# Last 512-token tile's second layer: other buffers for squares and reciprocals, and the older block's quotient ahead of the newer block's polynomials

## The chip, the core and the metric

The kernel runs on one core of a Trainium2 chip. The engines are PE (TensorE, matrix products), DVE (VectorE), ACT (ScalarE), POOL (GpSimd) and SP (which issues the transfers). Each works through its own queue in order, and they meet at semaphores. The metric is the device time of one launch in microseconds (us).

## What is computed

An attention without softmax (squared ReLU of the scores) gives 6016 rows of 256 values. A first feed-forward layer with ELU follows, and then the second one, whose activation is a rational function of the hidden value h. The change touches this last part:

```python
h = x @ w_in                       # 256 -> 2048
P = a[0] + a[1]*h + a[2]*h2 + a[3]*h3
Q = 1.0 + abs(b[0])*abs(h) + abs(b[1])*h2
g = P / (Q + 1e-06)
return g @ w_out                   # 2048 -> 256
```

## The kernel before

Tokens of the two feed-forward layers are taken in 13 tiles: one of 384, ten of 512 and two of 256 (`NFT` is 13, so tile `NFT - 3`, number 10 counted from 0, is the last with 512 tokens). The hidden dimension of 2048 is cut into blocks of 128 hidden units by up to 512 columns: a 512-token tile has 16 blocks, and a 256-token tile has 8, each with two groups of hidden units side by side. Every product is made of three matmuls on a high and a low part, so each block of either layer costs PE six matmuls of 512 columns for the hidden values (`hidden`, L358 to L361) and six for the projection (`mm3`, L239 to L241), or twelve and twelve of 256 columns.

`ffn_step(n)` writes the instructions of one step in a fixed order, and nothing rearranges them later. In the steps here, PE works on the first layer of tile 11 (every second step) while the second layer of tile 10 goes through, one block per step, in several stages: `second_hidden(j)` in one step, the polynomials of that block (`j1`) in the next, its reciprocal and quotient (`j2`) in the step after, its projection (`j4`) two steps later. I call `j2` the older block and `j1` the newer one, and number the blocks of tile 10 from 0 to 15. A step with a first-layer block I call a full step, one without it a half step.

Tile 10 uses the form "spread" of the activation:

- ACT: `linear` (L431), `square` (L439), `size` (L448), all from h in PSUM; later `recip`, a logarithm (L471) and an exponential (L472).
- POOL: `cubic` (L451), from linear and square; later `rest` (L485), the low part of the result. POOL also makes the low part of the first layer's block (L398).
- DVE: `denominator` (L457), from square and size; `numerator` (L465), from cubic; `quotient` (L478, L479, L480); and for the first layer `first_elu` (L391).

The buffers matter. Square and reciprocal of a block live in the two halves of one `raw` buffer, from `square` until `rest` has read the reciprocal. There are three `raw` buffers, and `load_x1` keeps one for the input of the last tile, from the step of the third first-layer block of tile 11 until `split_x1` in the step of its eighth. `e` (three buffers) holds the first layer's exponentials, and `r` (two) the reciprocals of the other tiles. The eight PSUM banks hold four accumulators and up to four hidden blocks; a block of the second layer frees its bank when its quotient is done, one of the first layer when its ELU is done.

After the last step, `finish` writes the last tile's second layer in an order that it plans itself; the change leaves that alone.

Of the kernel before, what the change touches and what calls it, by code (L numbers as in the profile page):

```python
# [16 lines left out]
def f(ap):  # L17
    return ap.bitcast(F32)
# [3 lines left out]
def attention_then_two_ffns(  # L22
# [51 lines left out]
    NFT = len(ftiles)  # L74
# [11 lines left out]
    def sb(tag, bufs, dt=F32, name=None):  # L86
        return sp.tile([P, W], dt, tag=tag, bufs=bufs, name=name or tag)

    def bank(name):
        return ps.tile([P, W], F32, tag="bank", name=name)  # L90
# [43 lines left out]
    def load_raw():  # L134
        return sp.tile([P, 2, 2 * P, 2], U32, tag="raw", bufs=3, name="raw")
# [187 lines left out]
    def load_x1(ti):  # L323
        t0, w = ftiles[ti]
        x1[ti] = load_raw().rearrange("p k f t -> p k (f t)").bitcast(F32)
        for sp_, (bb, i0, ws) in enumerate(spans):
            c0 = bb * S + i0
            lo, hi = max(c0, t0), min(c0 + ws, t0 + w)
            if lo < hi:
                nc.sync.dma_start(out=x1[ti][:, :, lo - t0:hi - t0], in_=xd[sp_][:, :, lo - c0:hi - c0])  # L330
# [11 lines left out]
    def flat(i):  # L342

        return PER[i[0]] * widths[i[0]]
# [34 lines left out]
    def first_hidden(i):  # L379
        g1[i] = hidden(0, x1[i[0]], i)  # L380

    def first_exp(i):
        h = g1[i]
        e = sb("e", 3)[:, :flat(i)]
        nc.scalar.activation(e, h, AF.Relu, scale=-1.0)
        nc.scalar.activation(e, e, AF.Exp, scale=-1.0)  # L386
        g1[i] = e, h

    def first_elu(i):
        e, h = g1[i]  # L390
        nc.vector.scalar_tensor_tensor(out=e, in0=e, scalar=-1.0, in1=h, op0=ALU.add, op1=ALU.max)  # L391
        g1[i] = e
# [8 lines left out]
    def split_x2(ti):  # L401
        w = widths[ti]
        x2[ti] = []
        for d in range(ND):
            p = acc[0, ti][d][:, :w]
            hi, lo = (sb("x2", 4, F32R)[:, :w] for _ in range(2))
            nc.scalar.copy(hi, p)
            nc.vector.tensor_tensor(out=lo, in0=p, in1=f(hi), op=ALU.subtract)
            x2[ti].append((hi, lo))

    def second_hidden(i):
        mid[i] = {"h": hidden(1, x2[i[0]], i)}

    def second(i, form):

        st = mid[i]  # L420
        h, n = st["h"], flat(i)
        last, plain = form == "last", form == "plain"
        v, act, tt, stt = nc.vector, nc.scalar.activation, nc.gpsimd.tensor_tensor, nc.vector.scalar_tensor_tensor

        def new(key, tag, bufs, dt=F32):
            t = wp.tile([P, W], dt, tag="w", name=tag) if last else sb(tag, bufs, dt)
            st[key] = t[:, :n]
            return st[key]

        def linear():  # L430
            act(new("p", "t", 3), h, AF.Identity, bias=a2, scale=a3)  # L431

        def square():
            if last:
                new("s", "s2", 0), new("r", "r", 0)
            else:
                raw = load_raw().rearrange("p k f t -> p k (f t)").bitcast(F32)
                st["s"], st["r"] = raw[:, 0, :n], raw[:, 1, :n]
            act(st["s"], h, AF.Square)  # L439

        def size():
            if last:
                st["q"] = bank("q")[:, :n]
            else:
                new("q", "q", 3)
            if plain:
                new("r", "r", 2)
            act(st["q"], h, AF.Abs, scale=b1 if plain else b0)  # L448

        def cubic():  # L450
            tt(out=st["p"], in0=st["p"], in1=st["s"], op=ALU.mult)  # L451

        def denominator():
            if plain:
                stt(out=st["q"], in0=st["q"], scalar=b0, in1=h, op0=ALU.add, op1=ALU.mult)  # L455
            else:
                stt(out=st["q"], in0=st["s"], scalar=b1, in1=st["q"], op0=ALU.mult, op1=ALU.add)  # L457

        def numerator():
            if plain:  # L460
                v.tensor_tensor(out=st["p"], in0=st["p"], in1=h, op=ALU.mult)
                stt(out=st["p"], in0=st["p"], scalar=a1, in1=h, op0=ALU.add, op1=ALU.mult)
                st["top"] = st["p"]
            else:
                stt(out=h, in0=h, scalar=a1, in1=st["p"], op0=ALU.mult, op1=ALU.add)  # L465
                st["top"] = h

        def recip():
            if plain:
                act(st["q"], st["q"], AF.Abs)  # L470
            act(st["r"], st["q"], AF.Ln, bias=NQ * LNS, scale=LNS)  # L471
            act(st["r"], st["r"], AF.Exp, bias=LNB, scale=-1.0)  # L472

        def quotient():

            new("hi", "x", 6, F32R)
            prod = st["q"] if plain else st["s"]
            stt(out=st["hi"], in0=st["top"], scalar=a0, in1=st["r"], op0=ALU.add, op1=ALU.mult)  # L478
            stt(out=prod, in0=st["q"], scalar=NQ, in1=f(st["hi"]), op0=ALU.add, op1=ALU.mult)  # L479
            stt(out=st["p"], in0=st["top"], scalar=a0, in1=prod, op0=ALU.add, op1=ALU.subtract)  # L480

        def rest():

            new("lo", "x", 6, F32R)
            tt(out=st["lo"], in0=st["p"], in1=st["r"], op=ALU.mult)  # L485
            g2[i] = st["hi"], st["lo"]

        if plain:
            return [
                ("linear", "A", 1.1, ["hidden"], linear),  # L490
                ("size", "A", 1.0, ["hidden"], size),
                ("denominator", "V", 1.0, ["size"], denominator),
                ("numerator", "V", 2.0, ["linear"], numerator),
                ("recip", "A", 2.6, ["denominator"], recip),
                ("quotient", "V", 3.0, ["recip", "numerator"], quotient),
                ("rest", "G", 1.8, ["quotient"], rest),
            ]
        return [
            ("square", "A", 0.85, ["hidden"], square),
            ("size", "A", 1.0, ["hidden"], size),  # L500
            ("linear", "A", 1.1, ["hidden"], linear),
            ("denominator", "V", 1.0, ["square", "size"], denominator),
            ("cubic", "G", 1.8, ["square", "linear"], cubic),
            ("recip", "A", 1.75, ["denominator"], recip),
            ("numerator", "V", 1.0, ["cubic"], numerator),
            ("quotient", "V", 3.0, ["recip", "numerator"], quotient),
            ("rest", "G", 1.8, ["quotient"], rest),
        ]

    def form(i):  # L510

        return "spread" if i[0] == NFT - 3 or i[0] == 0 and i[1] < 2 else "plain"

    def second_steps(i, *names):
        ops = mid[i].setdefault("ops", {x[0]: x[-1] for x in second(i, form(i))})
        for name in names:
            if name in ops:
                ops[name]()
# [32 lines left out]
    def ffn_step(n):  # L551
        i, i1, p = begun.get(n), begun.get(n - 1), projected.get(n)
        j, j1, j2, j4 = (second_begun.get(n - k) for k in (0, 1, 2, LAG2))
        last = p is not None and p[1] == NG[p[0]] - 1
        if i and i[1] * PER[i[0]] == 4 and i[0] + 1 < NFT:
            load_x1(i[0] + 1)

        if last and j:
            second_hidden(j)
        if p:  # L560
            project(0, p, g1.pop(p))
        if i:
            first_hidden(i)
        if j1:
            second_steps(j1, "linear", "square", "size", "cubic", "denominator")
            if form(j1) == "plain":
                second_steps(j1, "numerator")
        if i1:
            first_elu(i1)
        if i and i[1] == NG[i[0]] - 1 and i[0] + 1 < NFT:  # L570
            split_x1(i[0] + 1)
        early = n < LAG1 + NG[0] + 2
        if i1 and early:
            first_split(i1)
        if j2:
            second_steps(j2, "recip")
        if last:
            split_x2(p[0])
        if i:
            first_exp(i)  # L580
        if j2:
            second_steps(j2, "quotient", "rest")
        if j1 and form(j1) != "plain":
            second_steps(j1, "numerator")
        if i1 and not early:
            first_split(i1)
        if j4:
            second_project(j4)
            if j4[1] == NG[j4[0]] - 1:
                store(j4[0])  # L590
        if not last and j:
            second_hidden(j)
# [90 lines left out]
    first = stages_z(0, 0, True, True, False)  # L683
# [74 lines left out]
```

## Time and profile before

| | |
|---|---|
| median of 3 runs | 1644.72 us (1644.67 to 1645.53) |
| the profiled execution | 1644.66 us |
| its span, first to last instruction | 1642.9 us |
| PE busy | 97% of the span |
| DVE, ACT, POOL busy | 87%, 82%, 42% |
| mean granted TensorE clock | 0.993 |

The profiled execution is within 0.1 us of the median, and 1.8 us of it lie outside the span. In the trace, a row of an engine's timeline has its start, its duration, the engine, the line of the program, the operation, what it writes and reads, and in brackets how long the engine had been idle before it and what ended that. Matmuls are pipelined, so their work is read from the distance between starts. Instructions of DVE and ACT overlap their neighbours by up to 0.1 us too; so here again a cost in a row of instructions is the distance of two starts, and the duration counts where another engine waits for the end.

### The profile page before, as it was taken

To read this page: it belongs to the slowest core of one execution; us is meant where nothing else is said; L and a number is where in the kernel's file an instruction comes from. 1 tells how busy PE (TensorE), PEld (TensorE's weight loads), DVE (VectorE), ACT (ScalarE), POOL (GpSimd) and SP (SyncE) were. 2 spreads that over 40 slices of the span, in tenths; PEclk is the share of its full clock that TensorE was granted. 3 is DMA by queue.
4 is the path that set the end of the run, shared out by engine and by line. 5 is a ranking of instruction groups with operands and counts; after the bars stand their busy time and mean duration, and the time that the engine had idled before them with its cause. 6 is when DMAs were issued, how large, how long until landed. Compare 5 with 4: busy or idle time off the path is not lost.

```text
span 1642.9 us, 21580 instructions
## 1 busy us (share of the span) xinstructions
PE 1596.4 (97%) x7272; PEld 1312.4 (80%) x7272; DVE 1424.3 (87%) x2184; ACT 1342.0 (82%) x2297; POOL 687.9 (42%) x547
## 2 busy tenths in 40 slices
PE   8999999999999999999999999999999999987896
PEld 6888888888889988878788787878787878876796
DVE  8888889999997478898888989898989888896888
ACT  7777787878876788888898888888888989875786
POOL 3223230323322444444444445444445444454645
PEclk9999999999999999999999999999999999998999
DMA  4133333221221500000000000000000000000000
GB/s 128 62 119 104 115 117 111 84 82 61 70 84 60 165 14 1 23 1 27 1 26 1 26 1 1 26 1 26 1 27 0 20 1 20 1 2 12 1 14 14
DMA packets 42191, 67.72 MB, mean 41 GB/s; under 512 B 6112, under 2 KB 19168, under 8 KB 42080
## 3 DMA queue, kind: packets, MB, share of 16 engines
q1 hardware_dynamic: 42080, 66.34, 12.9%
q8 instruction: 57, 0.93, 0.3%
q14 instruction: 54, 0.44, 0.1%
HBM read 47.71 MB, written 18.61 MB: 40 GB/s over the span
## 4 chain that ended last, share of the span: by engine, by line
PE 81%; DVE 9%; ACT 4%; issue 3%; POOL 2%; DMA 0%; POOLq 0%; SPq 0%; DVEq 0%; ACTq 0%
PE acc L240 16%; PE acc L241 16%; PE acc L239 16%; PE h L358 9%; PE h L361 9%; PE h L359 9%; PE s L264 4%; PE s L263 4%; DVE x L478 2%; POOL x L485 1%; DVE e L391 1%; DVE t L480 1%; ACT q L448 1%; PE acc L301 1%; DVE s L273 1%
## 5 line engine op out<-in xcount | busy, mean ns | idle before, releaser
L485 POOL TENSOR_TENSOR x<-t,r 128x512 fp32r<-128x512 f32 (+1 forms) x174 | 222.6, 1279 | 475.3 <-DVE t L480 453.8
L398 POOL TENSOR_TENSOR lo<-e,hi 128x512 fp32r<-128x512 f32 (+1 forms) x192 | 246.8, 1286 | 25.5 <-ACT hi L397 23.3
L266 ACT ACTIVATE e<-s 128x512 f32<-128x512 f32 (+1 forms) x288 | 169.0, 587 | 92.1 <-PE s L264 87.2
L273 DVE SCALAR_TENSOR_TENSOR s<-s,e 128x512 f32<-128x512 f32 (+1 forms) x280 | 191.5, 684 | 46.5 <-ACT e L266 43.1
L431 ACT ACTIVATE t<-h,coef 128x512 f32<-128x512 f32 (+1 forms) x192 | 148.0, 771 | 86.9 <-PE h L361 86.8
L455 DVE SCALAR_TENSOR_TENSOR q<-q,coef,h 128x512 f32<-128x512 f32 (+1 forms) x166 | 122.1, 736 | 83.1 <-ACT q L448 82.9
L358 PE MATMUL h<-x,w 128*128 128x512 f32 (+2 forms) x416 | 156.5, 380 | 14.2 <-DVE t L480 13.2
L240 PE MATMUL acc<-x,w 128*128 128x512 f32 (+2 forms) x416 | 157.2, 378 | 9.6 <-POOL x L485 9.4
L240 PE MATMUL acc<-lo,w 128*128 128x512 f32 (+2 forms) x416 | 157.2, 378 | 2.9 <-POOL lo L398 2.6
L239 PE MATMUL acc<-x,w 128*128 128x512 f32 (+2 forms) x416 | 156.1, 375 | 3.2 <-ACT xo L531 3.2
L358 PE MATMUL h<-rl,w 128*128 128x512 f32 (+2 forms) x416 | 154.5, 375 | 4.4 <-DVE e L391 3.9
L239 PE MATMUL acc<-hi,w 128*128 128x512 f32 (+2 forms) x416 | 156.2, 376 | 0.0
L241 PE MATMUL acc<-x,w 128*128 128x512 f32 (+2 forms) x416 | 156.2, 375 | 0.0
L241 PE MATMUL acc<-hi,w 128*128 128x512 f32 (+2 forms) x416 | 155.8, 374 | 0.0
L359 PE MATMUL h<-x,w 128*128 128x512 f32 (+2 forms) x416 | 155.4, 377 | 0.0
L359 PE MATMUL h<-rl,w 128*128 128x512 f32 (+2 forms) x416 | 153.3, 372 | 0.0
L391 DVE SCALAR_TENSOR_TENSOR e<-e,h 128x512 f32<-128x512 f32 (+1 forms) x192 | 128.5, 669 | 23.8 <-ACT e L386 23.8
L397 ACT CAST hi<-e 128x512 fp32r<-128x512 f32 (+1 forms) x192 | 115.3, 600 | 34.1 <-DVE e L391 34.0
L478 DVE SCALAR_TENSOR_TENSOR x<-t,coef,r 128x512 fp32r<-128x512 f32 (+1 forms) x166 | 133.7, 806 | 0.1
L240 PE MATMUL acc<-lo,v 128*128 128x512 f32 (+1 forms) x334 | 130.9, 392 | 0.6 <-DVE lo L286 0.5
L448 ACT ACTIVATE q<-h,coef 128x512 f32<-128x512 f32 (+1 forms) x192 | 129.1, 672 | 2.4 <-DVE s L479 2.4
L239 PE MATMUL acc<-hi,v 128*128 128x512 f32 (+1 forms) x334 | 130.5, 391 | 0.0
(107 smaller groups left out, 4293.5 us busy)
## 6 DMA issues: line engine op xcount, KB each, us to landing
raw<-w_in_dram SPq DMA_DIRECT2D x16, 512.0 KB, 4.2
raw<-w_out_dram SPq DMA_DIRECT2D x16, 512.0 KB, 4.6
wd<-q SPq DMA_DIRECT2D x24, 256.0 KB, 2.2
raw<-wd SPq DMA_DIRECT2D x12, 512.0 KB, 3.4
raw<-v_dram SPq DMA_DIRECT2D x22, 256.0 KB, 3.3
raw<-uT_dram SPq DMA_DIRECT2D x10, 512.0 KB, 4.1
xd<-xo SPq DMA_DIRECT2D x20, 256.0 KB, 2.4
outT_dram<-xo SPq DMA_DIRECT2D x20, 256.0 KB, 2.2
```

Source lines behind the costliest of these rows:

```text
L239: nc.tensor.matmul(out, lhsT=lh, rhs=rh, start=start, stop=False)
L240: nc.tensor.matmul(out, lhsT=lh, rhs=rl, start=False, stop=False)
L241: nc.tensor.matmul(out, lhsT=ll, rhs=rh, start=False, stop=stop)
L266: nc.scalar.activation(p[:, :w], s[:, :w], AF.Relu, scale=SCALE)
L273: nc.vector.scalar_tensor_tensor(out=q[:, :w], in0=s[:, :w], scalar=SCALE, in1=p[:, :w], op0=ALU.mult, op1=ALU.mult)
L358: nc.tensor.matmul(h[:, cols], lhsT=wh[:, d, c], rhs=x[d][0], start=d == 0, stop=False)
L359: nc.tensor.matmul(h[:, cols], lhsT=wl[:, d, c], rhs=x[d][0], start=False, stop=False)
L361: nc.tensor.matmul(h[:, cols], lhsT=wh[:, d, c], rhs=x[d][1], start=False, stop=d == ND - 1)
L398: nc.gpsimd.tensor_tensor(out=lo, in0=e, in1=f(hi), op=ALU.subtract)
L431: act(new("p", "t", 3), h, AF.Identity, bias=a2, scale=a3)
L478: stt(out=st["hi"], in0=st["top"], scalar=a0, in1=st["r"], op0=ALU.add, op1=ALU.mult)
L485: tt(out=st["lo"], in0=st["p"], in1=st["r"], op=ALU.mult)
```

## The change

For the blocks of tile 10 (`late`), `square` takes a buffer of `e` and one of `r` and none of `raw`. In the steps whose older or newer block is of tile 10 (`turned`), the numerator of the older block comes first, then the first layer's ELU, the older block's reciprocal and quotient, and only then the polynomials of the newer block, which for tile 10 go square, size, linear, cubic, denominator. No instruction is added or removed.

```diff
@@ -433,6 +433,9 @@
         def square():
             if last:
                 new("s", "s2", 0), new("r", "r", 0)
+            elif late(i):
+
+                new("s", "e", 3), new("r", "r", 2)
             else:
                 raw = load_raw().rearrange("p k f t -> p k (f t)").bitcast(F32)
                 st["s"], st["r"] = raw[:, 0, :n], raw[:, 1, :n]
@@ -507,9 +510,13 @@
+    def late(i):
+
+        return i is not None and i[0] == NFT - 3
+
     def form(i):
 
-        return "spread" if i[0] == NFT - 3 or i[0] == 0 and i[1] < 2 else "plain"
+        return "spread" if late(i) or i[0] == 0 and i[1] < 2 else "plain"
@@ -561,10 +568,18 @@
         if i:
             first_hidden(i)
-        if j1:
-            second_steps(j1, "linear", "square", "size", "cubic", "denominator")
-            if form(j1) == "plain":
-                second_steps(j1, "numerator")
+        def polynomials():
+            if j1:
+                first = ("square", "size", "linear") if late(j1) else ("linear", "square", "size")
+                second_steps(j1, *first, "cubic", "denominator")
+                if form(j1) == "plain":
+                    second_steps(j1, "numerator")
+
+        turned = late(j1) or late(j2)
+        if not turned:
+            polynomials()
+        elif late(j2):
+            second_steps(j2, "numerator")
         if i1:
             first_elu(i1)
@@ -576,11 +591,15 @@
             second_steps(j2, "recip")
         if last:
             split_x2(p[0])
+        if turned:
+            if j2:
+                second_steps(j2, "quotient")
+            polynomials()
         if i:
             first_exp(i)
         if j2:
-            second_steps(j2, "quotient", "rest")
-        if j1 and form(j1) != "plain":
+            second_steps(j2, "rest") if turned else second_steps(j2, "quotient", "rest")
+        if j1 and form(j1) != "plain" and not late(j1):
             second_steps(j1, "numerator")
```

On DVE, one full step before, in which block 3 is the older (its q is 14696) and block 4 the newer (q 14758), and the start of the next one. The number behind a name tells one use of a buffer from another.

```order
L457 SCALAR_TENSOR_TENSOR q_14758<-raw_14756,coef_72,q_14758 128x512
L478 SCALAR_TENSOR_TENSOR x_14767<-h_14685,coef_72,raw_14694 128x512
L479 SCALAR_TENSOR_TENSOR raw_14694<-q_14696,x_14767 128x512
L480 SCALAR_TENSOR_TENSOR t_14692<-h_14685,coef_72,raw_14694 128x512
L465 SCALAR_TENSOR_TENSOR h_14722<-h_14722,coef_72,t_14754 128x512
L457 SCALAR_TENSOR_TENSOR q_14791<-raw_14789,coef_72,q_14791 128x512
L391 SCALAR_TENSOR_TENSOR e_14764<-e_14764,h_14741 128x512
```

The same step on DVE after the change (block 3 has q 14705, block 4 has q 14767; lines have moved by 3, so the denominator is L460, the numerator L468 and the quotient L481 to L483).

```order
L481 SCALAR_TENSOR_TENSOR x_14760<-h_14687,coef_72,r_14703 128x512
L482 SCALAR_TENSOR_TENSOR e_14702<-q_14705,x_14760 128x512
L483 SCALAR_TENSOR_TENSOR t_14707<-h_14687,coef_72,e_14702 128x512
L460 SCALAR_TENSOR_TENSOR q_14767<-e_14764,coef_72,q_14767 128x512
L468 SCALAR_TENSOR_TENSOR h_14725<-h_14725,coef_72,t_14769 128x512
L391 SCALAR_TENSOR_TENSOR e_14773<-e_14773,h_14744 128x512
```

The denominator of the newer block has moved from ahead of the older block's quotient to behind it, directly ahead of its own numerator.

On ACT, the same step before: three instructions for block 4, two for block 3, then the first layer's exponential (L385, L386).

```order
L431 ACTIVATE t_14754<-h_14722,coef_72 128x512
L439 ACTIVATE raw_14756<-h_14722 128x512
L448 ACTIVATE q_14758<-h_14722,coef_72 128x512
L471 ACTIVATE raw_14694<-q_14696 128x512
L472 ACTIVATE raw_14694<-raw_14694 128x512
L385 ACTIVATE e_14764<-h_14741 128x512
L386 ACTIVATE e_14764<-e_14764 128x512
```

And after the change.

```order
L474 ACTIVATE r_14703<-q_14705 128x512
L475 ACTIVATE r_14703<-r_14703 128x512
L442 ACTIVATE e_14764<-h_14725 128x512
L451 ACTIVATE q_14767<-h_14725,coef_72 128x512
L431 ACTIVATE t_14769<-h_14725,coef_72 128x512
L385 ACTIVATE e_14773<-h_14744 128x512
L386 ACTIVATE e_14773<-e_14773 128x512
```

The reciprocal of the older block now stands ahead of the newer block's three, whose order is square, size, linear. On POOL the order is the same in both kernels (cubic of the newer block, rest of the older one, then every second step the first layer's low part), and so is PE's.

## Rows read from the trace of the kernel before

**Rows 1.** The page's first line.

```profile
span 1642.9 us, 21580 instructions
```

**Rows 2.** Busy time by stretch: length, then PE, PEld, DVE, ACT, POOL; granted clock.

```profile
1400.00:1450.00 50.00, 50.00 (x222) 40.44 (x221) 43.88 (x67) 42.43 (x72) 23.88 (x19) 1.00 0.00 1
1485.60:1499.10 13.50, 10.52 (x50) 8.59 (x49) 9.30 (x12) 7.74 (x13) 6.37 (x5) 0.87 0.00 1
```

**Rows 3.** Waits from 1450 to 1550 us: total us, times, longest.

```profile
ACT raw L439 <- POOL x L485: 20.7, 9, 2.5
DVE q L457 <- ACT q L448: 19.0, 11, 2.0
```

**Rows 4.** Timeline of ACT, one full step: start, duration, line, [idle before].

```profile
1486.99 0.60 ACT L439 ACTIVATE raw<-h 128x512 f32<-128x512 f32 x1 [2.33 <-POOL x L485]
1487.48 0.68 ACT L448 ACTIVATE q<-h,coef 128x512 f32<-128x512 f32 x1
1488.05 0.63 ACT L471 ACTIVATE raw<-q 128x512 f32<-128x512 f32 x1
1488.71 0.63 ACT L472 ACTIVATE raw<-raw 128x512 f32<-128x512 f32 x1
1489.25 0.58 ACT L385 ACTIVATE e<-h 128x512 f32<-128x512 f32 x1
1490.40 0.76 ACT L431 ACTIVATE t<-h,coef 128x512 f32<-128x512 f32 x1
1493.68 0.60 ACT L439 ACTIVATE raw<-h 128x512 f32<-128x512 f32 x1 [2.52 <-POOL x L485]
```

**Rows 5.** Timeline of DVE in the same step.

```profile
1488.20 1.82 DVE L457 SCALAR_TENSOR_TENSOR q<-raw,coef,q 128x512 f32<-128x512 f32 x1 [2.03 <-ACT q L448]
1489.94 0.74 DVE L478 SCALAR_TENSOR_TENSOR x<-h,coef,raw 128x512 fp32r<-128x512 f32 x1
...
1491.44 0.75 DVE L480 SCALAR_TENSOR_TENSOR t<-h,coef,raw 128x512 f32<-128x512 f32 x1
1492.11 0.75 DVE L465 SCALAR_TENSOR_TENSOR h<-h,coef,t 128x512 f32<-128x512 f32 x1
```

**Rows 6.** Timeline of POOL, first beside block 0, then in the same step.

```profile
1462.53 1.75 POOL L398 TENSOR_TENSOR lo<-e,hi 128x512 fp32r<-128x512 f32 x1
...
1488.17 1.30 POOL L451 TENSOR_TENSOR t<-t,raw 128x512 f32<-128x512 f32 x1
...
1494.35 1.28 POOL L451 TENSOR_TENSOR t<-t,raw 128x512 f32<-128x512 f32 x1 [0.71 <-ACT raw L439]
```

**Rows 7.** Timeline of DVE around the first block of tile 10.

```profile
1461.37 1.76 DVE L457 SCALAR_TENSOR_TENSOR q<-raw,coef,q 128x512 f32<-128x512 f32 x1 [0.26 <-ACT q L448]
...
1464.87 1.67 DVE L479 SCALAR_TENSOR_TENSOR q<-q,x 128x512 f32<-128x512 f32 x1
...
1469.83 0.74 DVE L478 SCALAR_TENSOR_TENSOR x<-h,coef,raw 128x512 fp32r<-128x512 f32 x1
```

**Rows 8.** Timeline of DVE, blocks 10 to 12.

```profile
1533.86 1.40 DVE L457 SCALAR_TENSOR_TENSOR q<-raw,coef,q 128x512 f32<-128x512 f32 x1
...
1535.78 0.74 DVE L478 SCALAR_TENSOR_TENSOR x<-h,coef,raw 128x512 fp32r<-128x512 f32 x1
...
1538.61 1.44 DVE L457 SCALAR_TENSOR_TENSOR q<-raw,coef,q 128x512 f32<-128x512 f32 x1
```

**Rows 9.** Timeline of PE: a wait, and starts of groups of matmuls.

```profile
1492.25 0.69 PE L358 MATMUL h<-x,w 128*128 128x512 f32 x1 [2.98 <-DVE t L480]
...
1536.07 0.41 PE L239 MATMUL acc<-hi,w 128*128 128x256 f32 x1
...
1554.17 0.40 PE L239 MATMUL acc<-x,w 128*128 128x512 f32 x1
...
1555.57 0.28 PE L239 MATMUL acc<-hi,w 128*128 128x256 f32 x1
...
1556.97 0.28 PE L358 MATMUL h<-rl,w 128*128 128x256 f32 x1
```

## The prediction

> **What bounds the kernel now.** I read the stretches first: they show where PE, which carries most of the work, isn't full. From 1400 to 1450 us PE is busy without a gap at full clock; in the 13.5 us from 1485.6, two steps of the change's stage, it is busy 10.52 us at a granted clock of 0.87, and no other engine is full either [rows 2]. So something serial bounds this stage. The waits name it: ACT's square waits for POOL's `rest` nine times, 20.7 us in all, and DVE's denominator behind it for ACT, 19.0 us [rows 3].
>
> The timelines then show the loop. The square of the newer block starts at 1486.99, after 2.33 us of idle ACT, and size 0.49 later [rows 4]. The denominator starts at 1488.20 and holds DVE until the older block's quotient starts at 1489.94; its third instruction ends at 1491.44 + 0.75 = 1492.19 [rows 5]. `rest` follows on POOL (nearly 1.3 us), and at 1493.68 comes the next square, 6.69 us after the last [rows 4]. It needs that `rest` because the last tile's input holds one of three `raw` buffers, so two are left for two blocks. From block 0 to block 10 the first quotient instruction moves from 1469.83 to 1535.78, 65.95 us in ten steps, 6.60 each [rows 7, 8]. After that the third buffer is back, and two denominators stand 1538.61 - 1533.86 = 4.75 apart, in the old order still [rows 8]: the nearest row for a pace without that wait.
>
> PE's own need is lower. Six matmuls of 512 columns take 1555.57 - 1554.17 = 1.40 us, twelve of 256 columns 1556.97 - 1555.57 = 1.40 [rows 9]. A half step has two such groups (2.8), a full step four (5.6): 4.2 per step on average.
>
> **The change part by part.** The count and form of instructions stay, and no transfer is moved past another: the last tile's input is still loaded in the same step, and SP's queue is the same. Cost of work: nothing.
>
> *The buffers.* With square and reciprocal out of `raw`, square no longer waits for `rest` of the block before. The new owners: `r` has two buffers, and a reciprocal's was last read one step and more before. `e` has three for three uses in two steps, and a square's comes free with its block's quotient, in time. The first layer's exponential in a full step needs the buffer that POOL's low part of the half step before gives back; that comes out below.
>
> *The new loop.* I count from the start of an older block's quotient, 0. From ACT to DVE I take a hop of 0.04 (size ends at 1487.48 + 0.68 = 1488.16, the denominator starts at 1488.20). The exponential, 0.63 long, thus started at -0.67. ACT goes on: square 0.54 after that start (L472 to L385), at -0.13; size 0.49 later, 0.36; linear 0.57 later (L448 to the next), 0.93; it ends 0.76 later, 1.69 [rows 4]. POOL's cubic starts 0.07 behind ACT's end (1494.35 against 1493.68 + 0.60) and takes 1.28: until 3.04 [rows 4, 6]. DVE's quotient is 1.50 to its third instruction and 0.67 on, so the denominator can start at 2.17 [rows 5].
>
> It can't run there. The trace shows it beside the same POOL instruction: the denominator issued at 1488.20, 0.03 after POOL's cubic, lasts 1.82 us and ends at 1490.02, 0.55 after the cubic's end at 1489.47 [rows 5, 6]. Both read only SBUF operands; the quotient's first and third instructions, which read h in PSUM, take 0.74 and 0.75 [rows 5]. So the new denominator ends at 3.04 + 0.55 = 3.59. The logarithm follows after a hop, the exponential 0.66 after it, 0.63 long [rows 4], and a hop: the next quotient starts at 3.59 + 0.04 + 0.66 + 0.63 + 0.04 = **4.96**. The Trainium skill ("SBUF — State Buffer", "SBUF: two separate sides") says that such a pair of instructions of VectorE and GpSimd excludes each other for the whole instruction. Read literally, the loser's whole 0.75 would follow POOL's end, 0.20 more per step and 2.0 us in ten; the row's 0.55 decides against that.
>
> Numerator (0.67) and ELU fit between denominator and quotient: 3.59 + 0.67 + 0.67 = 4.93, just. POOL's `rest` waits for the denominator's end and lasts until about 4.8, the first layer's low part until 6.1, 1.1 into the next step; the exponential that needs its buffer comes at linear + 0.67 = 1.61 there, so that wait is covered by 0.5 us. So a step is 4.96 us, near the 4.75 above.
>
> *Sum, part 1: block 0.* Before, in its first step DVE's denominator (until 1461.37 + 1.76 = 1463.13) stands ahead of three instructions of the last plain block. Now these move up one place: they stand behind the same POOL instructions and end where the one before them ended, the third at 1464.87 + 1.67 = 1466.54 [rows 6, 7]. Denominator 0.67 to 0.75, logarithm, exponential and two hops 1.37: quotient of block 0 at about 1468.6, instead of 1469.83 [rows 7]: **1.2 us**.
>
> *Part 2: blocks 0 to 10.* Ten steps of 4.96 and an estimated 0.3 for the last plain tile's store on ACT and the last tile's split on DVE: 49.9 instead of 65.95, **16.05 us**. Block 10's quotient comes at 1518.5 instead of 1535.78.
>
> *Part 3: the hand-over.* Before, PE started its next full step at 1536.07, 0.3 after that quotient, having been kept waiting [rows 8, 9]. Now PE's last hidden block of the half step waits only for block 9's quotient (1513.5 + 2.25, so 1515.8), takes 1.4, and the full step starts at 1517.2, 1.3 ahead of block 10's quotient: **1.6 us** more, 18.85 in all. The three steps from there to 1555.57 took 19.50 [rows 9]. Their work is 5.6 + 4.2 + 5.6 = 15.4. PE will be held twice: the second of them starts when block 11's quotient is done (1518.5 + 4.96 + 2.25 = 1525.7), 2.9 after PE has emptied its queue (1517.2 + 5.6), and a hidden block waits some 0.8 for block 12's quotient. 15.4 + 2.9 + 0.8 = 19.1: **0.4 us** gained. A gap of 2.98 is followed at 1492.25 by a first matmul of 0.69 against 0.40 at full clock [rows 9]; I charge **0.5 us** for the lower of the two clock levels after the 2.9 (between 0 and 1.5). From there PE has no long wait before, and the pace is its own.
>
> Sum: 1.2 + 16.05 + 1.6 + 0.4 - 0.5 = 18.75 us. The profiled execution is 1644.66, its span 1642.9 [rows 1], the median of three 1644.72; 1644.7 - 18.75 = **1626.0 us**.
>
> **The rivals.**
>
> *Rest goes first.* When cubic ends, both DVE's denominator and POOL's `rest` are ready. If POOL's went first, the denominator would wait 1.25 more and the step be 6.2: 12 us lost, 1638. Against it: at 1462.53 POOL's next instruction was issued while the denominator had been waiting since 1461.37, and it lasted 1.75, so DVE went first [rows 6, 7]. 9%.
>
> *No collision.* If cubic comes after the denominator's start (ACT delayed by half a microsecond would do), the step is 2.17 + 0.75 + 1.37 = 4.29, close to PE's 4.2: some 7 us more, 1619. Against it: linear ends at 1.69, the denominator can't start before 2.17. 8%.
>
> *Nothing to see.* The gain could be given back later: if blocks 11 to 15 were held by a new wait. That would be the `e` ring: in full steps in a row a square waits for POOL's low part of the step before, a loop of 1.82 on ACT, three POOL instructions of 1.28 and two hops, 5.8, with the collision 6.35, against PE's 5.6. It holds about three steps, some 2 us, and would need all of 18.75: 1644.7. 5%.
>
> *Slower: PE's clock.* A pair of steps is 8.4 us of PE at the full level (2.4 GHz) and 16.8 at the lower (1.2). Before, the granted clock was 0.87 in such a pair [rows 2]. Should the changed stage with its shorter but still regular gaps be held at the lower level throughout, five pairs of 16.8 instead of 13.2 make 18 us more: 1663. It decides from the point where PE's pair passes 13.2, which needs 4.8 of its 8.4 us at the lower level. For it: there are gaps in every pair still, 2 x 4.96 - 8.4 = 1.5 us. Against: the stage has fewer and shorter ones, and with larger ones the clock fell only for a part. 4%.
>
> **How the numbers follow.** My forecast has 74%, from 1621 to 1633: 2.0 for the whole-duration reading, 1.0 for the clock after the gap, another 3.0 if PE's catching up after the store or the `e` ring costs more are the upper end; half of the 0.67 per step of the missing collision and 1.6 us of PE's held time the lower one. With the second rival the range is 1619 to 1633, which leaves out 18%. A difference of 0.2% (3.3 us) is about what a measurement can tell from none: faster 91% (forecast and the first two), same 5%, slower 4%.
>
> **What would show it.** Right: ACT's square waits for POOL no more between 1460 and 1530; quotients 4.9 to 5.1 us apart; the denominator lasts about 1.4 us (2.17 to 3.59), ending 0.55 after cubic; PE's long gaps in half steps go, the granted clock there rises toward 1.0. Wrong: a new wait of square or of the first layer's exponential for POOL in the ten steps; a `rest` that ends before the denominator; a pace of 4.3 or above 5.5; a wait of over 3 us on PE after block 10.

## The result and the profile after

The changed kernel takes 1629.87 us (median of 4 runs, 1628.25 to 1631.42) against 1645.12 us for the kernel before (4 runs, 1644.67 to 1646.42): a ratio of 0.9906, 95% interval 0.9889 to 0.9923. That is 15.3 us, or 0.9%, faster. I had predicted 1626.0, from 1619 to 1633.

The profiled run of the changed kernel is the slowest of its four, 1631.42 us. Here square is L442, size L451, cubic L454, logarithm and exponential of the reciprocal L474 and L475, and rest L488. First the span, against [rows 1]:

```profile
span 1629.6 us, 21604 instructions
```

Then the busy time by stretch, with the columns of [rows 2]: the plain tiles, two steps of the changed stage, and the two stretches after PE's long gaps.

```profile
1400.00:1450.00 50.00, 50.00 (x222) 40.45 (x221) 43.93 (x66) 42.65 (x72) 23.18 (x19) 1.00 0.00 1
1491.50:1501.70 10.20, 9.88 (x57) 8.30 (x57) 9.20 (x12) 7.68 (x14) 7.31 (x6) 1.00 0.00 1
...
1480.00:1490.00 10.00, 10.00 (x51) 8.50 (x51) 8.99 (x12) 8.19 (x15) 7.06 (x5) 0.87 0.14 52
1520.00:1530.00 10.00, 7.82 (x39) 7.15 (x40) 9.02 (x11) 5.86 (x11) 6.54 (x5) 0.83 0.00 0
```

Two steps now take 10.2 us instead of 13.5, PE is busy for 9.88 of it at full clock, and DVE is busy for 9.20, the most of any engine but PE. The waits of the same 100 us as in [rows 3]:

```profile
POOL t L454 <- ACT t L431: 22.8, 14, 2.1
ACT r L474 <- DVE q L460: 18.3, 12, 2.9
...
DVE x L481 <- ACT r L475: 4.8, 8, 0.8
...
PE acc L239 <- DVE t L483: 3.1, 1, 3.1
```

Both lines of [rows 3] are gone: ACT's square waits for POOL's `rest` no more, and DVE's denominator waits for ACT no more. Now ACT's logarithm waits for the denominator, and in every second step the quotient for ACT's exponential. That is the loop of the prediction. One turn of it in DVE's, ACT's and POOL's timelines, against [rows 4 to 6]:

```profile
1492.05 0.75 DVE L481 SCALAR_TENSOR_TENSOR x<-h,coef,r 128x512 fp32r<-128x512 f32 x1
...
1494.23 1.50 DVE L460 SCALAR_TENSOR_TENSOR q<-e,coef,q 128x512 f32<-128x512 f32 x1
1495.65 0.75 DVE L468 SCALAR_TENSOR_TENSOR h<-h,coef,t 128x512 f32<-128x512 f32 x1
1497.15 0.75 DVE L481 SCALAR_TENSOR_TENSOR x<-h,coef,r 128x512 fp32r<-128x512 f32 x1 [0.75 <-ACT r L475]
```

```profile
1492.97 0.78 ACT L431 ACTIVATE t<-h,coef 128x512 f32<-128x512 f32 x1
...
1495.82 0.63 ACT L474 ACTIVATE r<-q 128x512 f32<-128x512 f32 x1 [1.57 <-DVE q L460]
1496.49 0.63 ACT L475 ACTIVATE r<-r 128x512 f32<-128x512 f32 x1
```

```profile
1493.89 1.29 POOL L454 TENSOR_TENSOR t<-t,e 128x512 f32<-128x512 f32 x1 [2.04 <-ACT t L431]
1495.14 1.75 POOL L488 TENSOR_TENSOR x<-t,r 128x512 fp32r<-128x512 f32 x1
```

Linear starts 0.92 after the quotient and the cubic 0.92 after that. The denominator is issued 2.18 after the quotient, beside the cubic; it ends at 1495.73, 0.55 behind the cubic's end at 1495.18. The next quotient starts 5.10 after the last; the step after that takes 5.04.

For the sum I need the stage's beginning and end. The last common instruction ahead of it is the first layer's ELU on DVE, in the kernel before and in the changed one:

```profile
1458.26 0.68 DVE L391 SCALAR_TENSOR_TENSOR e<-e,h 128x512 f32<-128x512 f32 x1
```

```profile
1461.40 0.68 DVE L391 SCALAR_TENSOR_TENSOR e<-e,h 128x512 f32<-128x512 f32 x1
...
1471.76 0.75 DVE L481 SCALAR_TENSOR_TENSOR x<-h,coef,r 128x512 fp32r<-128x512 f32 x1 [0.16 <-ACT r L475]
...
1524.14 0.75 DVE L481 SCALAR_TENSOR_TENSOR x<-h,coef,r 128x512 fp32r<-128x512 f32 x1
```

In this execution the stage begins 3.14 us later, in work that the change doesn't touch. That isn't the change: when the same kernel was run again, this ELU came at 1458.28 and the time was 1628.15 us.

```profile
1458.28 0.68 DVE L391 SCALAR_TENSOR_TENSOR e<-e,h 128x512 f32<-128x512 f32 x1
```

In the ten profiles of this document it comes between 1458.26 and 1461.40; what moves it isn't shown. So the profiles' difference of 1644.66 - 1631.42 = 13.24 us is a gain of 16.4 in the stage less 3.1 lost ahead of it. The last two rows of the changed kernel above are the quotients of blocks 0 and 10. The group of PE's matmuls that stands at 1555.57 in [rows 9] is here:

```profile
1542.30 0.28 PE L239 MATMUL acc<-hi,w 128*128 128x256 f32 x1
```

### The profile page after: what moved, and what is told of

The parts are those of the page before. It is cut to its first block, busy times and chain, and to the rows that moved or that the text cites. A ratio compares the mean times of both kernels' runs of the same rounds, so it can differ in the third digit from the quotient of the medians.

```text
span 1629.6 us, 21604 instructions
## 1 busy us (share of the span) xinstructions
PE 1592.6 (98%) x7272; PEld 1310.2 (80%) x7272; DVE 1424.4 (87%) x2184; ACT 1340.3 (82%) x2297; POOL 691.1 (42%) x547
## 4 chain that ended last, share of the span: by engine, by line
PE 86%; DVE 8%; ACT 4%; issue 2%; POOL 1%; DMA 0%; POOLq 0%; SPq 0%; DVEq 0%; ACTq 0%
PE acc L240 17%; PE acc L241 17%; PE acc L239 16%; PE h L359 9%; PE h L361 9%; PE h L358 9%; PE s L264 4%; PE s L263 4%; DVE x L481 1%; DVE q L460 1%; DVE t L483 1%; DVE e L391 1%; PE acc L301 1%; ACT r L474 1%; DVE e L482 1%
## 5 line engine op out<-in xcount | busy, mean ns | idle before, releaser
L488 POOL TENSOR_TENSOR x<-t,r 128x512 fp32r<-128x512 f32 (+1 forms) x190 | 249.8, 1315 | 479.6 <-DVE t L483 453.9
L358 PE MATMUL h<-x,w 128*128 128x512 f32 (+2 forms) x416 | 154.0, 374 | 5.6 <-DVE t L483 5.5
L359 PE MATMUL h<-x,w 128*128 128x512 f32 (+2 forms) x416 | 153.9, 374 | 0.0
L474 ACT ACTIVATE r<-q 128x512 f32<-128x512 f32 (+1 forms) x190 | 118.5, 624 | 25.1 <-DVE q L460 19.5
L481 DVE SCALAR_TENSOR_TENSOR x<-t,coef,r 128x512 fp32r<-128x512 f32 (+1 forms) x166 | 133.5, 804 | 0.4 <-ACT r L475 0.4
L451 ACT ACTIVATE q<-h,coef 128x512 f32<-128x512 f32 (+1 forms) x192 | 128.8, 671 | 2.4 <-DVE s L482 2.4
```

What stands on the lines that cost most here:

```text
L358: nc.tensor.matmul(h[:, cols], lhsT=wh[:, d, c], rhs=x[d][0], start=d == 0, stop=False)
L359: nc.tensor.matmul(h[:, cols], lhsT=wl[:, d, c], rhs=x[d][0], start=False, stop=False)
```

## Experiments

All kernels below were timed beside the kernel before: the changed kernel again, its two halves and linear first against 1645.84 us (15 runs), the other four against 1645.37 us (9 runs). Intervals are 95%.

**The changed kernel again**, unaltered.

> The changed kernel as it is, to set beside the others on one chip. The first profile of it entered the changed stage 3.1 us later than the profile of before did (the ELU ahead of it at 1461.4 instead of 1458.3), in instructions that the change leaves alone. If that is chance, this profile enters near 1458 to 1460 and the median comes nearer to 1628; if it belongs to the kernel, it enters at 1461 to 1462 again and the median stays near 1630. From that ELU to the end: 168.2 us, within 0.5, either way.

Measured: 1628.26 us (1628.15 to 1628.75), ratio 0.9897 (0.9883 to 0.9910). Its profile enters the stage at 1458.28 and needs 168.1 us from there to the end, as expected. This is the time that I compare the variants with. Against the kernel before, timed beside it, it is 17.6 us faster.

**One half of the change each.** The first keeps the old order and takes the buffers; the second keeps `raw` and takes the new order.

```diff
 # buffers alone, on the kernel before
+            elif i[0] == NFT - 3:
+                new("s", "e", 3), new("r", "r", 2)
 # order alone, on the changed kernel
-            elif late(i):
-
-                new("s", "e", 3), new("r", "r", 2)
```

> Only the buffers of the change, the order as before. Theory (the wait for the third buffer is the loop, the order merely goes with it): square waits for POOL no more, DVE becomes the pace of the old order, 4.7 to 5.3 us a step as before had it for blocks 10 to 12; 1627 to 1632 us. Rival (the order is what breaks the loop): a step stays above 6 us, 1640 to 1645 us.

> Only the order of the change, squares and reciprocals in the raw buffers as before. In the new order square stands behind the older block's reciprocal, and the rest that frees its buffer was issued a step earlier: it ends 4.9 us after that step's quotient, when the next square is due. Theory (either part alone breaks the loop): steps of 5.0 to 5.3 us and 1628 to 1632 us. Rival (without the buffers nothing is won): square waits for POOL over 1.5 us a step again, 1640 to 1645 us.

Measured: the buffers alone give 1641.92 us, ratio 0.9978 (0.9969 to 0.9987); the order alone gives 1628.77, ratio 0.9901 (0.9887 to 0.9914). So the order brings the whole gain of this change, and beside it the buffers bring nothing that can be measured. The buffers alone come out at the rival's time, though not at its pace. The waits of the kernel with the buffers alone, from 1450 to 1550 us:

```profile
DVE q L459 <- ACT q L450: 11.2, 14, 3.8
...
ACT e L441 <- DVE t L482: 9.2, 10, 2.0
```

The square (L441 there) doesn't wait for `rest` now. It waits for the older block's quotient (L482), which gives its `e` buffer back and which the old order puts behind the newer block's denominator. Ten steps (quotient of block 0 at 1471.14, of block 10 at 1526.85) still shrink from 65.95 to 55.7, 5.57 each: neither the 4.7 to 5.3 of the theory nor the 6 and more of the rival. But behind block 12, where full steps follow each other, the quotients come at 1537.40, 1546.59, 1555.22 and 1563.27, more than 8 us apart; three such steps took 18.97 before (1546.49 to 1565.46) and take 25.87 now. Two of these quotients on DVE:

```profile
1537.40 0.74 DVE L480 SCALAR_TENSOR_TENSOR x<-h,coef,r 128x512 fp32r<-128x512 f32 x1
...
1546.59 0.73 DVE L480 SCALAR_TENSOR_TENSOR x<-h,coef,r 128x512 fp32r<-128x512 f32 x1
```

The timeline of ACT shows this step, starting with the first layer's exponential:

```profile
1539.75 0.60 ACT L385 ACTIVATE e<-h 128x512 f32<-128x512 f32 x1 [2.49 <-DVE t L482]
...
1542.92 0.60 ACT L441 ACTIVATE e<-h 128x512 f32<-128x512 f32 x1 [0.71 <-POOL lo L398]
...
1549.02 0.60 ACT L385 ACTIVATE e<-h 128x512 f32<-128x512 f32 x1 [3.22 <-PE h L361]
```

The exponential waits for a quotient and the square for POOL's low part: both wait for one of the three `e` buffers. The next exponential waits for PE, and PE has waited for the first layer's ELU, which stands on DVE behind a denominator that the late square held up:

```profile
1546.06 0.58 PE L358 MATMUL h<-rl,w 128*128 128x256 f32 x1 [3.28 <-DVE e L391]
```

Behind that gap PE's matmuls of 256 columns take 0.41 us instead of 0.28, at a granted clock of 0.50 from 1546 to 1551 us. A gain of some 10 us is thus largely given back, 6.9 us of it in these three steps. The ring of the `e` buffers starts this; how much is its own, and how much comes from PE's wait and its slower matmuls, no run separates. In the changed kernel the waits for this ring from 1450 to 1550 us are 1.3 us (the exponential, two waits) and 1.0 us (the square, two waits), and the kernel with the order alone, whose squares take no `e` buffer, isn't faster. With the order alone, the timelines of POOL and ACT show why the third `raw` buffer isn't missed:

```profile
1493.04 1.74 POOL L485 TENSOR_TENSOR x<-t,raw 128x512 fp32r<-128x512 f32 x1
```

```profile
1494.87 0.58 ACT L439 ACTIVATE raw<-h 128x512 f32<-128x512 f32 x1
```

`rest` ends at 1494.78, and the next square starts at 1494.87, when ACT has finished the exponential ahead of it. The steps are 5.05 us (block 1 at 1474.79, block 8 at 1510.12). So the new order moves the square to a place where its buffer has just come free.

**Was the `raw` buffer the limit in the old order?** The kernel before, with the last tile's input loaded four first-layer blocks later, so that three `raw` buffers are there for the first blocks of the stage.

```diff
-        if i and i[1] * PER[i[0]] == 4 and i[0] + 1 < NFT:
+        if i and i[1] * PER[i[0]] == (12 if i[0] == NFT - 2 else 4) and i[0] + 1 < NFT:
```

> The kernel before in its old order, with one edit: the last tile's input is loaded four first-layer blocks later, so that all three raw buffers are free for blocks 0 to 7 or so of the second layer (half of the ten slow steps or more) and only some steps have two. If the wait of the square for a raw buffer is by itself what sets 6.60 us per step, as I read the waits, the steps with three buffers fall to the 4.75 us seen behind block 10, and most of the stage's 16 us is gained without the new order: 1628 to 1634. If the order is what matters (the older block's quotient stands behind the newer block's denominator), as the runs with the buffers alone and the order alone suggest, some other wait takes the square's place and the time stays above 1638.

Measured: 1633.00 us, ratio 0.9926 (0.9913 to 0.9938). DVE's timeline, quotients of blocks 0, 6 and 7 and the denominator after it:

```profile
1470.03 0.74 DVE L478 SCALAR_TENSOR_TENSOR x<-h,coef,raw 128x512 fp32r<-128x512 f32 x1
...
1498.32 0.74 DVE L478 SCALAR_TENSOR_TENSOR x<-h,coef,raw 128x512 fp32r<-128x512 f32 x1
...
1505.01 0.74 DVE L478 SCALAR_TENSOR_TENSOR x<-h,coef,raw 128x512 fp32r<-128x512 f32 x1
...
1509.96 1.30 DVE L457 SCALAR_TENSOR_TENSOR q<-raw,coef,q 128x512 f32<-128x512 f32 x1 [2.04 <-ACT q L448]
```

Six steps with three buffers take 28.29 us, 4.72 each. As soon as the input holds its buffer, the step is 6.69 and the old wait is back. The reading of [rows 3] holds: that buffer was the limit, and freeing it is worth nearly 2 us a step without any new order. In these steps the old order is even faster than the changed kernel, whose steps average 5.07. It has the third buffer for six of the ten steps only, and six times 1.9 us are most of the 12.4 us that this kernel gains. Behind block 12, with the squares in `raw`, three steps take 18.96 here (1534.66 to 1553.62), as before: the 25.87 of the buffers alone belongs to the new buffers.

**The denominator beside the cubic.** Two kernels change only what runs beside it. In the first, linear goes ahead of square and size, which starts the cubic earlier. In the second POOL's cubic is left out for tile 10.

```diff
 # linear first
-                first = ("square", "size", "linear") if late(j1) else ("linear", "square", "size")
-                second_steps(j1, *first, "cubic", "denominator")
+                second_steps(j1, "linear", "square", "size", "cubic", "denominator")
 # no cubic
-                second_steps(j1, *first, "cubic", "denominator")
+                second_steps(j1, *first, *(() if late(j1) else ("cubic",)), "denominator")
```

> The change, but the newer block's three on ACT in the old order: linear, square, size. POOL's cubic can then start with square, about 0.6 us earlier, and the denominator that collides with it ends 0.6 us earlier. Theory (the collision of cubic and denominator sets the step): 4.4 to 4.5 us a step instead of 5.07, some 4 to 6 us less in all, PE's need of 8.4 us a pair being close: 1623 to 1626. Rival (the step is set by DVE and ACT alone, the collision is hidden): no difference from the change within 1 us.

> The changed kernel without POOL's cubic for tile 10: this multiplication is left out, everything else stays, and the numerator takes linear's result. If the denominator is held by the cubic that runs beside it, it lasts 0.74 to 0.8 us in nearly all steps instead of 1.43 to 1.51, the steps are 4.3 to 4.5 us instead of 5.07, close to PE's own need of 4.2, and the time is 1619 to 1623. If the denominator's length has another cause (its operands or the buffers they lie in), it stays at 1.4 and so does the time, 1627 to 1629.

Measured: linear first gives 1624.39 us (1624.05 to 1624.93), ratio 0.9873 (0.9860 to 0.9887); without the cubic it is 1619.90 (1618.60 to 1621.07), ratio 0.9847 (0.9833 to 0.9860). One turn with linear first, DVE and then POOL:

```profile
1480.07 0.75 DVE L481 SCALAR_TENSOR_TENSOR x<-h,coef,r 128x512 fp32r<-128x512 f32 x1 [0.59 <-ACT r L475]
...
1482.25 1.00 DVE L460 SCALAR_TENSOR_TENSOR q<-e,coef,q 128x512 f32<-128x512 f32 x1
...
1507.73 0.75 DVE L481 SCALAR_TENSOR_TENSOR x<-h,coef,r 128x512 fp32r<-128x512 f32 x1
```

```profile
1481.34 1.37 POOL L454 TENSOR_TENSOR t<-t,e 128x512 f32<-128x512 f32 x1 [1.97 <-ACT e L442]
```

And one without the cubic, on DVE:

```profile
1488.16 0.75 DVE L481 SCALAR_TENSOR_TENSOR x<-h,coef,r 128x512 fp32r<-128x512 f32 x1
...
1490.34 0.74 DVE L460 SCALAR_TENSOR_TENSOR q<-e,coef,q 128x512 f32<-128x512 f32 x1
...
1492.51 0.75 DVE L481 SCALAR_TENSOR_TENSOR x<-h,coef,r 128x512 fp32r<-128x512 f32 x1 [0.75 <-ACT r L475]
```

The denominator is issued 2.18 after the quotient in all three kernels. With linear first the cubic ends at 1482.71 and the denominator at 1483.25, 0.54 later, so it lasts 1.00, and six steps from 1480.07 take 27.66, 4.61 each. Without the cubic it lasts 0.74 and the step 4.35. With square and size first it is 1.50 and 5.10. So in these kernels the denominator's length follows the cubic's end, and the whole collision costs 1628.26 - 1619.90 = 8.4 us (some 8, since the kernel before was 0.5 us faster in the timing of the second). That removal also frees POOL of 16 instructions of some 1.3 us, so a part of it may be due to other work; linear first, which removes none, shows 3.9.

**Linear first with `raw`, and the split on ACT.** The first kernel takes the new order with linear first and without the new buffers. The second also moves the two casts that begin the last tile's split (L337) from DVE to ACT.

```diff
 # both: new order, linear first, squares and reciprocals in raw
-                new("s", "e", 3), new("r", "r", 2)
...
+                second_steps(j1, "linear", "square", "size", "cubic", "denominator")
 # the second also
-            nc.vector.tensor_copy(hi[d], raw[:, d])
+            (nc.scalar.copy if ti == NFT - 1 else nc.vector.tensor_copy)(hi[d], raw[:, d])
```

> The new order with squares and reciprocals still in raw, and for the newer block linear ahead of square and size. If the denominator's collision with POOL's cubic is what linear first takes away, denominators last about 1.0 us here too, the steps are 4.6 to 4.7 us, and the time is 1623 to 1625, like the run with linear first in the other buffers. If the other buffers were what allowed that pace, ACT's square waits for POOL's rest again and the time is 1627 or more.

> As the run before it, and the last tile's two casts from its input to the high part run on ACT instead of DVE. In the changed kernel these two took 2.03 us together on DVE beside POOL's work and the step around them 6.56 instead of 5.07 us. If that step's surplus is the casts' and what they push behind the next POOL instruction, it falls to below 5.5 and the time is 0.7 to 1.5 us under the run before it. If ACT, which is in the loop too, is held as long by them, there is no difference beyond 0.3 us.

Measured: 1623.55 us (1623.10 to 1624.24), ratio 0.9870 (0.9856 to 0.9883), and with the casts on ACT 1624.72 (1622.98 to 1625.18), ratio 0.9873 (0.9858 to 0.9889). The first is the fastest of the kernels that leave no work out. Against linear first in the new buffers (1624.39) it is 0.8 us, too little to call. The casts on ACT bring nothing: the 0.7 to 1.5 us that I expected don't come, and the two profiles show where they go. The step from block 8 to block 9 does fall, from 6.06 (1507.31 to 1513.37) to 4.55 (1508.01 to 1512.56). PE's waits behind it, first with the casts on DVE, then on ACT:

```profile
1516.66 0.50 PE L358 MATMUL h<-x,w 128*128 128x512 f32 x1 [2.80 <-DVE t L480]
...
1525.62 0.39 PE L358 MATMUL h<-rl,w 128*128 128x256 f32 x1 [0.16 <-DVE t L480]
```

```profile
1515.19 0.50 PE L358 MATMUL h<-x,w 128*128 128x512 f32 x1 [0.73 <-DVE t L480]
...
1525.04 0.40 PE L358 MATMUL h<-rl,w 128*128 128x256 f32 x1 [2.54 <-DVE t L480]
```

The first gap nearly closes and the second opens. That one ends with block 11's quotient in both kernels, and behind it comes the slow clock in one of them. Busy time and granted clock in the 2.4 or 2.5 us after 1525.6 and 1525.0:

```profile
1525.60:1528.00 2.40, 2.38 (x16) 2.25 (x17) 2.28 (x4) 1.87 (x4) 2.04 (x2) 1.00 0.00 0
```

```profile
1525.00:1527.50 2.50, 2.46 (x12) 2.46 (x13) 2.39 (x4) 2.04 (x4) 2.02 (x2) 0.55 0.00 0
```

From the first of these matmuls to the projection of the next block PE takes 6.05 us with the casts on DVE (until 1531.67) and 7.25 with them on ACT (until 1532.29). With the casts on DVE the clock is low too, 0.73 in the 3.4 us after the first gap, but that stretch lies ahead of a point where PE has to wait for block 11's quotient anyway, and the wait left there is 0.16. With the casts on ACT that quotient comes 1.3 us earlier (counted from the common ELU, at 1459.76 and 1460.47), PE has emptied its queue before it, and the low clock, near its level of 1.2 GHz, falls where nothing covers it: 1.2 of the 1.3 us go there.

## Why the prediction was right, and where it was off

The time lies in the range and 3.9 us above the forecast; the rerun's median is 2.3 above it. The stage's gain was forecast as 18.75 and measured as 16.4 between the two profiles; the rerun's medians differ by 17.6. The measured parts are distances between the rows above and those of [rows 7 to 9]: from the ELU to block 0's quotient, from there to block 10's, and from there to PE's group, each before and after:

| part | forecast, us | measured, us |
|---|---|---|
| block 0 earlier, from the common ELU | 1.2 | 11.57 - 10.36 = 1.2 |
| ten steps, quotient of block 0 to block 10 | 16.05 | 65.95 - 52.38 = 13.6 |
| hand-over, steps after, clock | 1.6 + 0.4 - 0.5 = 1.5 | 19.79 - 18.16 = 1.6 |

**Block 0: right**, mechanism and size. The instructions moved up one place and the same POOL instructions ended them.

**The loop: right in its mechanism, 0.13 a step too short.** The steps are 5.04 and 5.10 against 4.96. Eight of the ten average 5.07; the one behind the split's, told below, takes 5.24; together the nine average 5.09. The denominator's end 0.55 behind the cubic's was right to 0.01: it is 0.55 with square and size first and 0.54 with linear first. The Trainium skill ("SBUF — State Buffer", "SBUF: two separate sides") says that the loser is fully blocked for the other's whole instruction. Read literally, with all of the denominator's 0.75 behind POOL's end, this would be 0.20 more for each collision, and the traces don't show that. The surplus in the eight is nearly all hops: the cubic started 0.14 behind linear's end instead of my 0.07, and in every second step the logarithm 0.09 behind the denominator instead of 0.04. Nine steps: 1.2 us, 0.9 of it in the eight.

**The step with the split: the term that was mis-sized.** It is the one from block 8 to block 9. For the last plain tile's store and the last tile's split I put down an estimate of 0.3, without working out what stands beside them. The split's step took 6.56 us, 1.3 more than the forecast's 4.96 + 0.3. DVE's and POOL's timelines of it in the changed kernel:

```profile
1516.61 2.03 DVE L337 CAST rl<-raw 128x256 fp32r<-128x256 f32 x2
...
1518.90 0.74 DVE L481 SCALAR_TENSOR_TENSOR x<-h,coef,r 128x512 fp32r<-128x512 f32 x1
1519.67 1.66 DVE L482 SCALAR_TENSOR_TENSOR e<-q,x 128x512 f32<-128x512 f32 x1
```

```profile
1515.44 1.75 POOL L488 TENSOR_TENSOR x<-t,r 128x512 fp32r<-128x512 f32 x1
1517.14 1.35 POOL L398 TENSOR_TENSOR lo<-e,hi 128x512 fp32r<-128x512 f32 x1
...
1519.53 1.26 POOL L454 TENSOR_TENSOR t<-t,e 128x512 f32<-128x512 f32 x1
```

The two casts, of SBUF operands only, stand beside two POOL instructions and take 2.03 us. In the kernel before they fell into a pause of POOL:

```profile
1530.30 0.48 DVE L337 CAST rl<-raw 128x256 fp32r<-128x256 f32 x2
```

So the quotient comes late; that is the 1.3. In the step behind it the quotient's second instruction, usually 0.69 to 0.76, meets the next cubic and takes 1.66, while the denominator, at 0.74, meets none: 5.24 in all. I had charged this price for the denominator and had not asked which other instructions of DVE without a PSUM operand the denser stage would bring beside POOL.

**The hand-over: right in its sum, not in its parts.** PE waited 3.50 us for block 9's quotient, which the split's step had delayed, and not 2.9 for block 11's; the two waits behind it were 0.64 and 0.52.

```profile
1522.18 0.50 PE L358 MATMUL h<-x,w 128*128 128x512 f32 x1 [3.50 <-DVE t L483]
```

I had charged 0.5 for the clock. It was 0.68 in the 3.9 us from 1522.1 and 0.92 in the next 5.6; what that cost by itself isn't measured. That the parts cancel was luck.

**What carried the gain: half right.** The prediction named the wait of the square for `rest`, and that was the limit in the old order (4.72 us a step with a third buffer). But it put the end of that wait down to the new buffers. They weren't needed: the new order alone gives 1628.77. And the buffers in the old order bring the `e` ring that I had weighed as a rival, at a higher price than I had worked out: 8.0 to 9.2 us in full steps, PE's wait and slower matmuls among them, against 5.8 to 6.35. In the new order its waits come to 2.3 us, near the some 2 us of the rival's own working, and cost nothing that the run with the order alone could show.

**The rivals.** `rest` did not go ahead of the denominator: in the turn above it was issued at 1495.14, while the denominator was still waiting, and took 1.75, until 1496.89, 1.16 behind the denominator's end. The clock rival fell: 1.00 from 1491.50 to 1501.70; only the two gaps of over 3 us were followed by stretches at 0.87 and 0.83. The time without a collision, worked out as 4.29 a step and 1619, was measured as 4.35 and 1619.9 by taking the cubic away.

## What to carry to other kernels

A wait for a buffer names an instruction that is late, and there are two cures: another buffer, or an order in which that instruction ends earlier. Try each alone, since another buffer may bring another ring, with a price elsewhere: here a third buffer of the old ring gave steps of 4.72 us, and buffers taken from another ring gave 5.57 and lost most of that again in the full steps. When an edit makes a stage denser, list every instruction that comes to stand beside another engine's on the same memory, the rare ones too (a split, a store): here the split's step cost 1.3 us more than its estimate, and the hops of the eight regular steps 0.9 together. A stall that is taken out of one step is only gained if the engine at the end of the chain doesn't empty its queue one step later.

## What the hardware showed that was not expected

- The blocked instruction ends 0.54 to 0.55 us behind POOL's end, wherever in POOL's instruction it was issued: 0.34 after its start (lasting 1.50) or 0.91 after it (lasting 1.00). It is 0.53 to 0.56 for every one of DVE's 128x512 instructions of over 0.9 us from 1460 to 1550 us, in all nine traces with the cubic.
- Two casts of 128x256 on DVE took 2.03 us beside two POOL instructions and 0.48 in a pause of POOL; on ACT, beside the same kind of POOL instruction, they took 0.73.
- After a gap of 2.54 us PE ran at a granted clock of 0.55 for 2.5 us. The same kind of slow stretch cost nothing visible where PE had to wait afterwards anyway, and 1.2 us where it didn't.
